# A linear-attention and MoE-block kernel: its whole instruction order written by hand, and the transposes of queries and the maxima of keys moved off TensorE

## The chip, the core and the metric

One core of a Trainium2 chip runs the whole program in one launch. The metric is device time in microseconds from start to end of an execution. TensorE (PE in the profile) multiplies, VectorE (DVE), ScalarE (ACT) and GpSimd (POOL) do elementwise work, SyncE (SP) issues the DMAs. Each engine works off its own queue in order and waits for others by semaphores.

## What is computed

```python
# q, k, v: 8 batches, 8 heads, 576 tokens, 64 wide;  w_in 512x2048, w_out 2048x512 (float64)
q_s = exp(q - max(q, axis=-1));  q_s = q_s / (sum(q_s, axis=-1) + 1e-9)   # softmax of a query over its 64
k_s = exp(k - max(k, axis=2));   k_s = k_s / (sum(k_s, axis=2) + 1e-9)    # softmax of keys over the 576 tokens
kv  = einsum('bhsd,bhse->bhde', k_s, v)                                   # one 64x64 matrix for each head
x   = einsum('bhsd,bhde->bhse', q_s, kv)                                  # as 4608 tokens x 512
h   = x @ w_in;  g = h - tanh(h);  out = g @ w_out                        # 4608 x 512
```

## The kernel before

The 4608 tokens are 36 tiles of 128, taken in nine chunks of four (512 tokens). For each chunk the hidden layer of 2048 is walked in 16 steps `f`, so there are 144 steps. A step is 12 matmuls `ph` (w_in times x, the matrices held in two parts each: high times high, high times low, low times high, four slices of 128 each) and 12 matmuls `po` (four token tiles, in each `gh` by the two parts of w_out and `gl` by the first one). Between the two lies the elementwise chain of the step: `u`, `t`, `m`, `vv` on ScalarE, `g`, `tt`, `gg`, `cp` on VectorE, then `gh` (ScalarE) and `gl` (GpSimd, in places VectorE). `ph` has two banks of PSUM, so `ph` of step n+2 cannot start before the last reader of step n's bank, `tt`, is done. The `po` of a step follows the `ph` of two steps later (`LAG = 2`).

Beside the steps runs the attention for the chunks to come. For each batch: load keys and values, maximum over tokens (`kv_max` on VectorE folds 576 tokens to 128 rows; four transposes `pm` on TensorE and a reduction `mx` give one column of maxima; `kv_rows`, tile `pb`, spreads it to all partitions by two 512-column matmuls with a diagonal `d`, built by GpSimd, in batches 2 to 7), `kv_sub`, `kv_exp`, 80 small matmuls `pk` (`kv_mm`), `kv_norm` into `kvs`. For each query tile: softmax (`q_max`, `q_sub`, `q_exp`, `q_sum`, `q_eps`, `q_inv`), `q_norm` (GpSimd), `q_turn` (four TensorE transposes into PSUM, tile `pt`), `q_keep` (ScalarE copies them to SBUF), and for each pair of tiles `x_mm` (matmuls `px`), of which `x_part` makes `xh` (ScalarE) and `xl` (VectorE).

The 64 left-over tokens of two batches form a tile of their own after every odd batch, so chunks and batches do not line up. `ORDER` writes out the order of all engines for the first 19 steps, in which the weights are also split into two parts (`cl`, `pr`, `lo`, `st`, `ca`, `sub`). After that only the queues of TensorE and SyncE are in written order (`prepare` puts each attention part at a half step); the program's scheduler orders the other three engines. `warm` words are idle matmuls ahead of the first step.

Of the kernel before, what the change touches and what calls it, by code (L numbers as in the profile page):

```python
# [31 lines left out]
ORDER = """  # L32
q1 q0 mq1 qu1 qe1 mq0 qu0* k0.0 k0.1 k0.2 km0.a ld.i2 km0.b warm4 km0.c km0.d sq1 qe0 pm0 cl.i2
vo0.0 pr.i2 vo0.2 mx0 ld.i1 lo.i2 sa1 mh0 sr1 ld.i0 ml0 vo0.1 cl.i1 ld.i4 pb0 qn2 v0.0 lo.i0 sq0
pt2 lo.i1 lo.i4 ks0.0 cl.i0 qs2 ke0.0 st.i2 qn3 sa0 q3 ks0.2 sr0 ks0.1 warm13 pk0.0 ca.i2 pt3
warm2 ke0.2 pr.i0 qn1 pt1 mq3 qn0 cl.i4 ke0.1 v0.1 st.i0 qu3* v0.2 pt0 pr.i1 pk0.1 pr.i4 qs0 ld.o0
vo1.1 pk0.2 ca.i0 qs3 st.i4 sl0 rs0 rc0 qe3 kn0 qs1 sub.i0 cl.o0 q2 sq3 st.i1 pr.o0 ld.i5 warm5
ld.i3 px0 mq2 sa3 cl.i5 vo1.2 px2 ca.i4 sub.i2 lo.o0 sub.i4 xh0.0 xh2.0 k1.0 xl0.0 ca.i1 xh2.1
xl2.0 xl2.1 ld.o2 xh0.1 lo.i3 k1.1 xl0.1 qu2 ld.o1 vo1.0 k1.2 lo.i5 v1.2 cl.i3 sub.i1 ld.i6 warm10
qe2 pr.i3 sr3 km1.a ph0 sq2 lo.o2 km1.b ld.i12 ph1 pr.i5 st.i3 qn6 m0 km1.c u0 t0 ld.o7 ld.i7 pt6  # L40
v1.0 cl.o1 km1.d vv0 ph2 ca.i3 g0 sa2 t1 tt0 qs6 lo.o1 u1 pr.o1 lo.i6 gg0 ld.o5 sr2 cp0 ld.o3 g1
u2 gh0 sub.i3 st.i5 cl.i12 ld.o10 pm1 mx1 m1 ph3 pr.i12 vv1 qn4 tt1 cl.i6 cl.o2 st.o0 gg1 mh1 v1.1
ph4 cl.i7 ml1 pb1 t2 pr.i6 ld.i9 pr.o2 ca.o0 cp1 ca.i5 st.i6 lo.i7 vv2 gl0 sub.i5 u3 ks1.0 qn5 gh1
ks1.1 t3 ks1.2 ke1.0 ld.i10 pt4 ke1.1 ke1.2 cl.o5 g2 ca.i6 st.o1 ca.o1 qs4 ph5 gl1 tt2 pk1.0 gg2
pk1.1 pk1.2 tt3 sub.o0 m2 po0.0 u4 qn7 ld.o13 cp2 g3 vv3 lo.o3 sl1 cl.o3 ld.i8 st.o2 ld.o4 sub.o1
m3 po0.1 po1.1 pt5 gg3 pr.i7 po0.2 qs5 po0.3 ca.o2 st.i7 vv4 ld.o6 cp3 ld.o8 sub.o2* gh2 t4 ld.i11
gl2* rs1 po1.3 sub.i6 pt7 m4 ca.i7 cl.o4 po1.0 po1.2 po2.1 u5 tt4 pr.o3 lo.o4 rc1 ld.i15 g4 po2.3
gh3 gg4 po2.2 st.o3 t5 ld.o12 cp4 kn1 sub.i7 lo.o5 po2.0 ca.o3 ld.o9 qs7 ph6 vv5 px4 gl3* gh4
pr.o5 sub.o3 pr.o4 u6 tt5 g5 po3.0 cl.o6 m5 st.o5 st.o4 cl.i9 po3.2 ld.o11 po3.1 xh4.1 ca.o4 xh4.0
t6 sub.o4 gg5 cp5 ca.o5 pr.o6 ld.i13 lo.i11 lo.o6 po3.3 xl4.1 gh5 lo.o7 xl4.0 tt6 vv6 ld.o15 ph7  # L50
gl4* t7 px6 xh6.1 cl.o10 st.o6 po4.2 lo.i15 g6 po4.1 sub.o5 cl.i10 gg6 po4.3 tt7 xl6.1 gl5 m6 cp6
xh6.0 po4.0 cl.o7 u7 po5.2 cl.o9 xl6.0 ca.o6 m7 ld.i14 po5.1 po5.0 g7 vv7 po5.3 ph8 sub.o6 pr.i9
gh6 cl.o8 cl.i11 lo.i12 pr.o7 gg7 ph9 cl.i15 cl.i8 cp7 st.o7 t8 gl6* u8 gh7 ca.o7 sub.o7 t9 g8
ld.o14 u9 po6.2 po6.0 tt8 po6.1 gl7* lo.i10 m8 vv8 po7.0 cl.o15 g9 tt9 po6.3 pr.i15 ph10 pr.i11
gg8 ev.0 cp8 cl.i14 cl.o11 lo.o10 m9 pr.o10 po7.2 vv9 gh8 sv.0 t10 u10 ph11 st.i15 st.o10 po7.3
gg9 cp9 lo.i8 tt10 cl.o12 ev.2 vv10 ca.o10 m10 gl8 st.i11 u11 po7.1 sub.o10 g10 ca.i15 po8.1 po8.0
gh9 pr.o8 gl9* cl.o13 gg10 t11 ev.3 ca.i11 ph12 cp10 ev.1 tt11 vv11 po9.1 g11 sub.i11 sv.1 pr.i10
po8.2 gg11 u12 st.i12 po8.3 gh10 po9.2 m11 gl10* po9.3 st.i10 t12 po9.0 g12 cp11 po10.1 ca.i12
pr.o12 ph13 ca.i10 tt12 po10.0 vv12 sub.i15* lo.o12 pr.i8 cl.o14 sub.i12 sub.i10 po10.2 gg12 lo.i9
m12 st.i8 ph14 st.i9 gh11 t13 cp12 u13 gl11* lo.o8 sv.3 ca.i8 vv13 lo.i14 po10.3 t14 tt13 g13 gh12  # L60
st.o12 m13 gg13 u14 po11.1 po11.0 po11.2 ph15 sub.i8 ca.o12 pr.i14 ca.i9 cl.i13 gl12 pr.o15
sub.o12 pr.o11 cp13 st.i14 po11.3 tt14 vv14 po12.1 t15 po12.3 g14 lo.o15 sub.i9 st.o8 m14 lo.o11
po12.2 ca.i14 gh13 sub.i14 gg14 ca.o8 cp14 st.o15 tt15 pr.o9 po12.0 gl13* ph16 u15 po13.2 lo.o9
st.o11 gh14 vv15 gl14* sub.o8 po13.1 po13.3 sv.2 ca.o15 st.o9 ca.o11 g15 u16 lo.i13 gg15 sub.o15
m15 g16 po13.0 ca.o9 po14.2 t16 cp15 pr.i13 po14.1 vv16 sub.o11 sub.o9* gh15 tt16 po14.0 st.i13
ph17 m16 lo.o13 u17 pr.o13 po14.3 gg16 vv17 gl15* ph18 po15.1 cp16 g17 gh16 po15.2 po15.0 m17 t17
po15.3 st.o13 gg17 gl16* t18 u18 lo.o14 po16.2 vv18 tt17 cp17 g18 po16.1 pr.o14 tt18 ca.o13 m18
gg18 ca.i13 gh17 st.o14 po16.3 sub.o13* cp18 po16.0 ca.o14 sub.i13* gh18 gl17* sub.o14* gl18*
# [765 lines left out]
```

## Time and profile before

| | |
|---|---|
| three runs | 894.58, 894.74, 894.89 us (median 894.74) |
| profiled execution | 894.5 us, its span 892.7 us, mean granted clock 0.998 |
| TensorE busy | 872.3 us, 98% of the span |
| VectorE, ScalarE, GpSimd busy | 610.8, 555.1, 301.6 us (68%, 62%, 34%) |
| DMA queue of SyncE | 56.63 MB, 20.6% of 16 engines' span |

The span starts and ends with the first and the last instruction; 1.8 us of the execution lie around it. Consecutive matmuls overlap in the records (a duration of 393 ns, a new one every 227 ns), so what TensorE needs for a piece of work is read from the distance between starts. A wait is time in which an engine stood idle, put down to what released it.

### The profile page before, as it was taken

How to read it: one execution, taken by the hardware profiler on the slowest of the kernel's cores; microseconds unless marked ns; L12 is line 12 of the kernel's file. 1: busy time of each engine (PE TensorE's matmuls, PEld its weight loads, DVE VectorE, ACT ScalarE, POOL GpSimd, SP SyncE). 2: the span in 40 equal slices, each digit the busy share in tenths (PEclk: the TensorE clock that was granted, in tenths of full speed). 3: DMA queues.
4: the chain of work that ended last, by engine and by line, in shares of the span. 5: the costliest groups of instructions: out<-in, count | busy, mean ns of one | idle time of the engine just before them, and what ended most of it. 6: DMA issues, size and time to landing. Idle time of an engine off the chain costs nothing.

```text
span 892.7 us, 13189 instructions
## 1 busy us (share of the span) xinstructions
PE 872.3 (98%) x5008; PEld 716.3 (80%) x5008; DVE 610.8 (68%) x897; ACT 555.1 (62%) x967; POOL 301.6 (34%) x255
## 2 busy tenths in 40 slices
PE   5899999999999999999999999999999999999997
PEld 4788878888878888888888888888888888888886
DVE  7899999856686767666756865765766466454454
ACT  5799987656465556565655564566555556556553
POOL 3463361533153324332433233323433233222221
PEclk9999999999999999999999999999999999999999
DMA  9991301130413011300240011401100020001001
GB/s 294 323 391 55 98 3 42 48 119 1 129 49 106 1 36 48 108 25 0 71 108 24 1 47 37 106 1 48 48 25 1 3 69 12 1 1 48 1 1 47
DMA packets 79775, 57.47 MB, mean 64 GB/s; under 512 B 14688, under 2 KB 72032, under 8 KB 79712
## 3 DMA queue, kind: packets, MB, share of 16 engines
q1 hardware_dynamic: 79712, 56.63, 20.6%
q8 instruction: 39, 0.64, 0.3%
q14 instruction: 24, 0.20, 0.1%
HBM read 46.14 MB, written 10.49 MB: 63 GB/s over the span
## 4 chain that ended last, share of the span: by engine, by line
PE 92%; DVE 3%; ACT 2%; DMA 1%; issue 1%; POOL 0%; SPq 0%; DVEq 0%; ACTq 0%; POOLq 0%
PE po L653 42%; PE ph L570 42%; PE pk L325 2%; PE pt L463 2%; PE px L489 2%; PE warm L202 1%; DMA q<-in_q_dram 1%; DMA k<-in_k_dram 1%; PE pb L299 0%; PE pb L283 0%; DVE km L252 0%; PE pm L261 0%; POOL d L293 0%; DMA out_dram<-back 0%; DVE mq L410 0%
## 5 line engine op out<-in xcount | busy, mean ns | idle before, releaser
L653 PE MATMUL po<-w_o,gh 128*128 128x512 f32 x1152 | 358.8, 393 | 0.0
L570 PE MATMUL ph<-xh,w_i 128*128 128x512 f32 x1152 | 311.9, 393 | 0.0
L610 POOL TENSOR_TENSOR gl<-g,gh 128x512 fp32r<-128x512 f32 x129 | 172.5, 1337 | 387.0 <-ACT gh L607 369.2
L653 PEld LDWEIGHTS po<-w_o,gh 128*128 128x128 f32 x1152 | 214.0, 188 | 47.0 <-issue 2.1
L570 PEld LDWEIGHTS ph<-xh,w_i 128*128 128x128 f32 x1152 | 213.8, 188 | 43.4 <-DVE mq L410 0.2
L591 DVE SCALAR_TENSOR_TENSOR g<-u,ph 128x512 f32<-128x512 f32 x144 | 98.1, 681 | 209.8 <-ACT t L585 201.1
L653 PE MATMUL po<-w_o,gl 128*128 128x512 f32 x576 | 224.7, 390 | 1.1 <-DVE gl L610 1.1
L607 ACT CAST gh<-g 128x512 fp32r<-128x512 f32 x144 | 89.4, 621 | 170.4 <-DVE g L604 164.7
L570 PE MATMUL ph<-xl,w_i 128*128 128x512 f32 x576 | 154.5, 390 | 0.0
L585 ACT ACTIVATE u<-ph 128x512 f32<-128x512 f32 x144 | 86.1, 598 | 75.6 <-PE ph L570 72.2
L599 DVE SCALAR_TENSOR_TENSOR g<-vv,g 128x512 f32<-128x512 f32 x144 | 117.9, 818 | 18.6 <-ACT vv L585 8.0
L653 PEld LDWEIGHTS po<-w_o,gl 128*128 128x128 f32 x576 | 108.1, 188 | 25.2 <-DVE gl L610 2.2
L570 PEld LDWEIGHTS ph<-xl,w_i 128*128 128x128 f32 x576 | 108.0, 188 | 23.4 <-DVE xl L510 0.2
L604 DVE COPY_PREDICATED g<-mk,t 128x512 f32<-128x512 int32 x144 | 122.3, 850 | 3.5
L585 ACT ACTIVATE mk<-ph 128x512 int32<-128x512 f32 x144 | 86.3, 599 | 36.1 <-DVE g L591 32.9
L585 ACT ACTIVATE vv<-u,b_pa 128x512 f32<-128x512 f32 x144 | 104.7, 727 | 0.0
L596 DVE TENSOR_TENSOR t<-ph,t 128x512 f32<-128x512 f32 x144 | 98.0, 680 | 1.5 <-ACT mk L585 1.5
L585 ACT ACTIVATE t<-ph 128x512 f32<-128x512 f32 x144 | 85.5, 595 | 0.9 <-PE ph L570 0.9
L449 POOL TENSOR_TENSOR qn<-q,sq 128x512 f32<-128x512 f32 x30 | 33.0, 1102 | 25.4 <-PE pt L463 12.8
L415 POOL TENSOR_TENSOR q<-q,mq 128x1024 f32<-128x1024 f32 x13 | 26.3, 2021 | 43.2 <-DVE mq L410 43.0
L410 DVE TENSOR_REDUCE mq<-q 128x16 f32<-128x1024 f32 x15 | 18.2, 1216 | 20.0 <-DMA q<-in_q_dram 19.9
L181 POOL TENSOR_TENSOR w_i<-c_i,w_i 128x512 fp32r<-128x512 f32 x14 | 20.2, 1448 | 28.5 <-ACT w_i L177 28.5
(94 smaller groups left out, 583.8 us busy)
## 6 DMA issues: line engine op xcount, KB each, us to landing
k<-in_k_dram SPq DMA_DIRECT2D x16, 512.0 KB, 5.6
raw_i<-in_moe_w_in_dram SPq DMA_DIRECT2D x16, 512.0 KB, 6.9
raw_o<-in_moe_w_out_dram SPq DMA_DIRECT2D x16, 512.0 KB, 8.1
q<-in_q_dram SPq DMA_DIRECT2D x15, 512.0 KB, 4.0
v<-in_v_dram SPq DMA_DIRECT2D x14, 512.0 KB, 4.9
out_dram<-o SPq DMA_DIRECT2D x28, 256.0 KB, 2.0
kr<-in_k_dram SPq DMA_DIRECT2D x8, 128.0 KB, 5.2
spare_v<-in_v_dram SPq DMA_DIRECT2D x2, 512.0 KB, 8.4
```

The costliest lines, as they stand in the source:

```text
L181: eng.tensor_tensor(w[:, 1], st["c"].bitcast(F32), w[:, 0].bitcast(F32), op=ALU.subtract)
L415: eng.tensor_tensor(qf, qf, mq, op=ALU.subtract)
L449: eng.tensor_tensor(qn.rearrange("p a g d -> p g a d"), qt[:, :, j].rearrange("p (g a) d -> p g a d", g=2), sq[:, :, j : j + 1] .broadcast ...
L570: nc.tensor.matmul(ph, w[:, i, c], x[:, c, :], start=(n == 0), stop=(n == len(ops) - 1))
L585: nc.scalar.activation(new(tag, **of), st[src], fn, **kw)
L591: nc.vector.scalar_tensor_tensor(new("g"), st["u"], C2, st["ph"], op0=ALU.mult, op1=ALU.mult)
L596: nc.vector.tensor_tensor(st["t"], st["ph"], st["t"], op=ALU.subtract)
L599: nc.vector.scalar_tensor_tensor(st["g"], st["vv"], PB, st["g"], op0=ALU.add, op1=ALU.mult)
L604: nc.vector.copy_predicated(st["g"], st["mk"], st["t"])
L607: nc.scalar.copy(new("gh", F32R), st["g"])
L610: eng.tensor_tensor(new("gl", F32R), st["g"], st["gh"].bitcast(F32), op=ALU.subtract)
L653: nc.tensor.matmul(po[t], g[:, cols], wt["o", f][:, w], start=(begin and n == 0), stop=(end and n == 2),)
```

## The change

- Every instruction of the five engines now stands in a written order: `FIRST` for the first 32 steps, `ROUND` once for each of chunks 2 to 8 (words with + prepare the next chunk and fall away where there is none), `LAST` for the end. A step's `ph` is cut in three words (`pha`, `phb`, `phc`, four matmuls each) and a tile's `po` in two (`a`: the two `gh` matmuls, `b`: the `gl` one), which need not be neighbours. A star puts a word on VectorE that otherwise goes to GpSimd.
- Queries of chunks 2 to 8: `q_scale` normalizes in place, two VectorE transposes (`q_blocks`, word `tb`) turn the tile within squares of 32x32, one DMA puts it in DRAM (`qp`), four DMAs fetch its squares back in their places (`qg`). `q_turn` and `q_keep` remain for chunks 0 and 1 only.
- Keys' maxima of batches 2 to 7: a VectorE transpose in squares (`kb`), a reduction (`kr`), three small ScalarE copies that bring quarters together (`kq`), a reduction and a transpose on VectorE (`kx`, `kt`), 2 KB to DRAM (`kp`) and back, spread over 128 partitions (`kg`). `kv_sub` then reads SBUF and may go to GpSimd. `pm`, `mx`, `mh`, `ml`, `d` and `pb` remain for batches 0 and 1 only.
- The left-over tokens of all batches form chunk 8, so chunk j is batch j; `kvs` is saved to DRAM for it (`kv_save`) and read back (`kv_again`).

```diff
-    tiles = []
-    for b in range(B):
-        tiles += [((b, u), j) for u in range(NKP) for j in range(2)]
-        if b % 2:
-            tiles.append(((b, "rest"), 0))
+    tiles = [((b, u), j) for b in range(B) for u in range(NKP) for j in range(2)]
+    tiles += [(("rest", m), j) for m in range(B // 4) for j in range(2)]
...
+    def q_blocks(i: int):
+        unit, j = tiles[i]
+        qt = qs_of[unit][:, :, j]
+        qs_of[i] = tb = ap.tile([P, 2, 2, NC, SQ], F32, name=f"tb{i}", tag="qs", bufs=3)
+        for g in range(2):
+            nc.vector.transpose(
+                tb[:, g],
+                qt[:, g * NC : (g + 1) * NC].rearrange("p a (s i) -> p s a i", s=2),
+            )
+
+    def q_put(i: int):
+        tb = qs_of[i]
+        nc.sync.dma_start(qd[i], tb.rearrange("p g s a t -> p (g s a t)"))
+
+    def q_get(i: int):
+        qs_of[i] = qs = ap.tile([P, NQ, NC, SQ], F32, name=f"qs{i}", tag="qs", bufs=3)
+        rows = qd[i].rearrange("(q i) (c n) -> i q c n", q=NQ, c=NQ)
+        for c in range(NQ):
+            nc.sync.dma_start(
+                qs[c * SQ : (c + 1) * SQ].rearrange("p q a t -> p q (a t)"), rows[:, :, c]
+            )
...
+    def kv_best_put(b: int, st: dict):
+        nc.sync.dma_start(kvm[b].rearrange("(c i) -> c i", i=SQ), st["rt"][:NB])
+
+    def kv_best_get(b: int, st: dict):
+        st["mrow"] = mrow = ap.tile([P, H, D], F32, name=f"mrow{b}", tag="qs", bufs=3)
+        nc.sync.dma_start(
+            mrow.rearrange("p h d -> p (h d)"), kvm[b].unsqueeze(0).broadcast_to([P, DM])
+        )
...
+ROUND = """
+pha0 +q.0 phb0 phc0 po14.0a po14.3a u0 t0 g0 po14.0b po15.0a pha1 phb1 vv0 phc1 +mq.0 po14.2a m0
+t1 pha2 po15.0b po14.3b gg0 po15.3a u1 po14.1a po14.2b m1 tt0 po15.2a po15.3b cp0 gh0 tt1 +qu.0
...
+po1.2b phb4 m3 t3 phc4 vv3 os.0 po0.1b t4 g2 po1.0b gg2 pha5 cp2 po1.1a +k.2 gh2 po1.1b po0.3b
+po1.3a phb5 po2.0a +sq.0 os.3 +sa.0 u4 +sr.0 g3 po1.3b tt3 phc5 po2.2a os.1 gg3 os.2 vv4 cp3 gl2*
+pha6 gh3 m4 po2.3a u5 po2.1a phb6 vv5 t5 po2.1b tt4 g4 phc6 gg4 +k.0 cp4 gl3* m5 po2.0b +k.1
++again gh4 +q.1 po2.2b g5 pha7 u6 tt5 t6 vv6 gg5 cp5 po3.0a po2.3b tt6 phb7 +km.a po3.0b +qn.1
+gl4* g6 phc7 po3.2a u7 po4.0a po4.0b +km.b m6 +qn.0 po3.1a t7 gh5 +km.c gg6 po3.3a cp6 po3.1b
+po3.2b po3.3b +km.d +kb pha8 po4.3a +tb.1 po4.2a phb8 g7 po4.1a phc8 po4.3b +tb.0 m7 +v.0 +kr gh6
+t8 po4.1b +kq.1 po4.2b tt7 po5.0a +kq.2 u8 +kq.3 +kx +qp.0 tt8 pha9 gl5 po5.0b vv7 +kt gg7 phb9
...
++sl u12 po9.0b m11 po9.3b gg11 tt12 gh10 +rs +rc po9.2a g12 pha13 vv12 +kn phb13 +tb.3
+po9.1a phc13 po9.2b cp11 po10.0a po9.1b gl10 +px.0 gh11 m12 po10.2a po10.0b gg12 po10.1a +tb.2 u13
++xh.0.0 pha14 po10.3a po11.0a t13 tt13 gl11 phb14 cp12 +qp.3 phc14 +qp.2 po10.1b po10.2b vv13
+po10.3b gh12 g13 m13 +xh.0.1 gl12 pha15 po11.3a po11.1a t14 gg13 phb15 po11.2a phc15 po11.0b
+po11.2b cp13 +xl.0.0 u14 po11.1b po11.3b po12.0a m14 g14 tt14 po12.2a +qg.3 vv14 po12.1a po12.3a
++qg.2 gh13 gg14 po12.1b +px.1 po12.0b +xl.0.1 u15 m15 t15 cp14 po12.3b +sv po12.2b vv15 po13.0a
++gl13* gh14 g15 gg15 +xh.1.1 po13.1a +xh.1.0 po13.2a tt15 cp15 gh15 gl14* +xl.1.0 po13.0b po13.3a
+po13.1b +xl.1.1 po13.3b gl15* po13.2b
+"""
+
+LAST = """
+po142 po143.0a po143.0b oc8.0 os8.0 po143.1a po143.1b oc8.1* os8.1 po143.2a po143.2b oc8.2 os8.2
+po143.3a po143.3b oc8.3* os8.3
```

## Rows read from the trace of the kernel before

**Rows 1.** The page: busy time of the engines (share of the span, number of instructions), and TensorE's busy tenths and granted clock in 40 equal slices of the span.

```profile
PE 872.3 (98%) x5008; PEld 716.3 (80%) x5008; DVE 610.8 (68%) x897; ACT 555.1 (62%) x967; POOL 301.6 (34%) x255
...
PE   5899999999999999999999999999999999999997
...
PEclk9999999999999999999999999999999999999999
```

**Rows 2.** All waits of TensorE: who waited for whom, us in total, times, longest.

```profile
PE pm L261 <- DVE km L255: 8.3, 1, 8.3
PE warm L202 <- DVE xl L510: 3.0, 1, 3.0
PE warm L202 <- POOL ident masks.py:199: 1.4, 1, 1.4
PE pb L283 <- DVE mh L270: 1.2, 1, 1.2
PE po L653 <- DVE gl L610: 1.1, 1, 1.1
PE pb L299 <- POOL d L293: 0.4, 1, 0.4
```

**Rows 3.** TensorE's timeline, chunk 6: start us, us, instruction. Starts of `ph`, `pt`, `pm`, `pb`, `px` and `pk` that bound single steps: a plain step (578.08 to 583.52), steps with a transposed query tile (583.52, 589.43), with a pair's `px` (595.36 to 602.08), with the keys' maxima (618.41, 624.34), with `pk` (630.28 to 637.03).

```profile
578.08 1.07 PE L570 MATMUL ph<-xh,w_i 128*128 128x512 f32 x4
...
583.52 0.60 PE L463 MATMUL pt<-ident,qn 128*128 128x128 f32 x4
...
589.43 0.60 PE L463 MATMUL pt<-ident,qn 128*128 128x128 f32 x4
...
595.36 1.07 PE L570 MATMUL ph<-xh,w_i 128*128 128x512 f32 x4
...
602.08 1.07 PE L570 MATMUL ph<-xh,w_i 128*128 128x512 f32 x4
...
618.41 0.60 PE L261 MATMUL pm<-ident,km 128*128 128x128 f32 x4
...
624.34 0.63 PE L299 MATMUL pb<-d,one_r 128*128 128x512 f32 x2
...
630.28 1.07 PE L570 MATMUL ph<-xh,w_i 128*128 128x512 f32 x4
...
637.03 1.07 PE L570 MATMUL ph<-xh,w_i 128*128 128x512 f32 x4
```

**Rows 4.** Groups of TensorE instructions by line: count, busy us, mean ns of one; idle before.

```profile
L463 PE MATMUL pt<-ident,qn 128*128 128x128 f32 x144 | 22.3, 279 | 0.0
...
L299 PE MATMUL pb<-d,one_r 128*128 128x512 f32 x12 | 4.0, 405 | 0.4 <-POOL d L293 0.4
```

**Rows 5.** Busy time by stretch (us from the span's start): length, then PE, PEld, DVE, ACT, POOL with instructions, granted clock, DMA share, GB/s.

```profile
60.00:80.00 20.00, 20.00 (x144) 15.50 (x142) 19.65 (x35) 19.61 (x38) 7.94 (x6) 1.00 0.40 153
...
300.00:390.00 90.00, 90.00 (x542) 73.69 (x541) 58.90 (x86) 53.28 (x94) 31.21 (x27) 1.00 0.17 48
```

**Rows 6.** Groups of VectorE instructions by line: count, busy us, mean ns of one; idle before and its releasers.

```profile
L596 DVE TENSOR_TENSOR t<-ph,t 128x512 f32<-128x512 f32 x144 | 98.0, 680 | 1.5 <-ACT mk L585 1.5
...
L604 DVE COPY_PREDICATED g<-mk,t 128x512 f32<-128x512 int32 x144 | 122.3, 850 | 3.5
...
L610 DVE TENSOR_TENSOR gl<-g,gh 128x512 fp32r<-128x512 f32 x15 | 11.0, 733 | 2.3 <-ACT gh L607 2.3
...
L410 DVE TENSOR_REDUCE mq<-q 128x16 f32<-128x1024 f32 x15 | 18.2, 1216 | 20.0 <-DMA q<-in_q_dram 19.9
...
L346 DVE TENSOR_TENSOR kvs<-pk,rs 128x256 f32<-128x256 f32 x8 | 3.4, 424 | 0.2
```

**Rows 7.** DMA issues by tile: number, KB each, median us from issue to landing.

```profile
q<-in_q_dram SPq DMA_DIRECT2D x15, 512.0 KB, 4.0
...
out_dram<-o SPq DMA_DIRECT2D x28, 256.0 KB, 2.0
...
q_rest<-in_q_dram SPq DMA_DIRECT2D x8, 128.0 KB, 3.1
```

**Rows 8.** SyncE's timeline between 487 and 553 us: start, time that the issue took.

```profile
487.05 0.37 SPq L395 DMA_DIRECT2D q<-in_q_dram  x1
...
551.42 1.36 SPq L384 DMA_DIRECT2D q_rest<-in_q_dram  x2
```

**Rows 9.** The timeline of all engines at the end: the last `ph`, `tt` of that step, and the weight loads of its first `po`.

```profile
878.20 1.07 PE L570 MATMUL ph<-xh,w_i 128*128 128x512 f32 x4
...
882.25 0.68 DVE L596 TENSOR_TENSOR t<-ph,t 128x512 f32<-128x512 f32 x1
...
884.49 0.30 PEld L653 LDWEIGHTS po<-w_o,gh 128*128 128x128 f32 x2 [0.21 <-ACT gh L607]
...
885.22 0.19 PEld L653 LDWEIGHTS po<-w_o,gl 128*128 128x128 f32 x1 [0.43 <-DVE gl L610]
```

**Rows 10.** The timelines of TensorE and VectorE in the first 36 us.

```profile
31.98 3.80 PE L202 MATMUL warm<-ident 128*128 128x128 f32 x20 [3.05 <-DVE xl L510]
...
35.43 1.59 PE L570 MATMUL ph<-xh,w_i 128*128 128x512 f32 x4
...
4.67 1.22 DVE L410 TENSOR_REDUCE mq<-spare_q 128x16 f32<-128x1024 f32 x1 [4.67 <-DMA spare_q<-in_q_dram]
...
31.25 2.47 DVE L510 TENSOR_TENSOR xl<-px,xh 128x512 fp32r<-128x512 f32 x4
```

More of the change, by code (lines that the diff above doesn't have):

```diff
@@ L38 @@
[L38 to L43, printed above, removed]
@@ L50 @@
[L50 to L55, printed above, removed]
@@ L56 @@
[L56 to L61, printed above, removed]
@@ L127, in attn_moe_kernel @@
     nc.gpsimd.tensor_copy(one_r, one)
+    SQ = 32
+    NQ = P // SQ
+    NB = DM // SQ
+    best = sm.tile([SQ, SQ], F32, name="best")
+    nc.gpsimd.memset(best, 0.0)
     kvs = [const.tile([P, NC, D], F32, name=f"kvs{i}") for i in range(3)]
@@ L585, in act, with ph @@
             nc.scalar.activation(new(tag, **of), st[src], fn, **kw)
-        def ph():
-            st["ph"] = h_mm(j, f)
+        def ph(part: int):
+            if "ph" not in st:
+                pool, tag = (ps_o, "o") if j == 0 and f in (2, 3) else (ps_h, "h")
+                st["ph"] = pool.tile([P, CH], F32, name=f"ph{j}_{f}", tag=tag)
+            w = wt["i", f].rearrange("p t (c f) -> p t c f", c=NC)
+            i, x = ((0, 0), (0, 1), (1, 0))[part]
+            for c in range(NC):
+                n = st["n"] = st.get("n", -1) + 1
+                nc.tensor.matmul(
+                    st["ph"], w[:, i, c], xs[j][x][:, c, :], start=n == 0, stop=n == 3 * NC - 1
+                )
         def g():
@@ new lines, in attn_moe_kernel, with go, many @@
+    ENG = mybir.EngineType
+    POOLED = {"qu", "qn", "gl", "sub", "ks"}
+    def go(name: str, fn):
+        kind = name.lstrip("+").split(".")[0].rstrip("0123456789*")
+        if name[-1] == "*":
+            fn(nc.vector)
+        elif kind in POOLED and not (kind == "ks" and name[0] != "+"):
+            fn(nc.gpsimd)
+        elif kind == "kq":
+            fn(nc.scalar)
+        else:
+            fn()
+    def many(name: str) -> list:
+        bare = name.rstrip("0123456789")
+        if "." in name or bare not in ("ph", "po"):
+            return [name]
+        if bare == "ph":
+            return [f"pha{name[2:]}", f"phb{name[2:]}", f"phc{name[2:]}"]
+        return [f"{name}.{t}{part}" for t in range(TPC) for part in "ab"]
@@ L805 @@
+    with tc.manual_schedule(engines={ENG.PE, ENG.DVE, ENG.Activation, ENG.Pool, ENG.SP}):
+        run(FIRST, 1)
+        for j in range(2, NCH):
+            run(ROUND, j)
+        run(LAST, 0)
 _INS = ["q", "k", "v", "moe_w_in", "moe_w_out"]
```

473 lines of the change are left out of this document (267 added, 206 removed).

## Prediction

> **What bounds the kernel now.** I read the page's busy line and slices first: TensorE is busy 98% of the span and at nine tenths or more in all slices but the first two and the last, at the full granted clock (the 2.4 GHz level); the others stand at 34 to 68% [rows 1]. Then the list of all its waits: 15.4 us, of which all but the last two entries (1.5 us) lie ahead of the first step [rows 2]. From the first `ph` at 35.43 us [rows 10] to the end the kernel is one unbroken stream of matmuls, and what a piece of work costs there is what it adds to the distance between starts. A plain step lasts 5.44 us (578.08 to 583.52) [rows 3], that is 24 matmuls of 0.2267 us. 144 steps are 783 us; the other 69 of the 852 us from the first `ph` to the last `po` are attention matmuls and the 1.5 us of waits. So the change is worth what it takes out of TensorE's stream, less every idle time that it puts there.
>
> **What it takes off TensorE.** A step with a transposed query tile lasts 5.91 us (583.52 to 589.43) and 5.93 (to 595.36): 0.48 more than a plain one. Four transposes a tile, 144 in all [rows 4], make 36 tiles; `q_turn` stays for 8, so 28 go: 28 x 0.48 = 13.4 us. The step with `pm` lasts 5.93 (0.49 more) and the one with `pb` 5.94 (0.50 more) [rows 3]; both go for six batches (12 `pb` of this form, two each [rows 4]): 6 x 0.99 = 5.9 us. Together 19.3 us. `pk` stays (1.31 more in the step from 630.28).
>
> **What stays on TensorE in another form.** `px` now reads its queries in runs of 32 columns and, in chunk 8, in pieces of 64. No row has runs of 32. The nearest: a pair of which one tile is in 64-column pieces adds 6.72 - 5.44 = 1.28 us (595.36 to 602.08) [rows 3], so I price every pair at that, and the change of form at 0; bounds -1 us and +6 us (14 pairs, each a third dearer). The cut of `ph` and `po` into words adds no instruction: 0, since every matmul loads its own weights already.
>
> **What it adds elsewhere, and its cover.** A round holds, on TensorE, 16 x 5.44 + 2 x 1.28 + `pk` 3.2 = 92.9 us. On VectorE:
> - Transposes `tb`: eight a round of 128x256. The trace has no VectorE transpose; the 128x256 `kvs` took 0.424 us, and the dearest per element, `copy_predicated`, 0.85 for 128x512 [rows 6]. I take 0.42 (same size), bounds 0.25 and 0.85: 3.4 us a round (2 to 7).
> - `kb` and `kr` about 0.7 each (a 128x512 pass is 0.68), `kx` and `kt`, of 64 and 32 columns, an estimated 0.2 each (half the 128x256 one): 1.8, in place of `mx`, `mh`, `ml`.
> - Eight `gl` with a star at 0.733 [rows 6] and two starred `qn` at 0.68: 7.2.
> With the steps' four passes (16 x 3.03 = 48.5), reductions, `km`, `ks`, `xl` and the rest by their means I come to 76 us of 92.9; a 90 us stretch before held 59 [rows 5]. ScalarE loses the `qs` copies and gains three small ones; GpSimd loses `d` and half of `gl`. All of that is hidden by TensorE as long as no wait ends last on it, which is the question of the next part.
>
> Two trips through DRAM are new. Count the matmuls between the words in a round, at 0.2267 us each. From `px.0`'s end (whose reading frees the buffer that `tb.2` writes) to `px.1` lie 12.5 us. In them fall `tb.2` (0.85), the store (2.0 for 256 KB [rows 7]), eight fetches queued on SyncE at about 0.4 to 0.7 each [rows 8], and the last landing (3.1 for a 128 KB load [rows 7]): 9 to 12 us, room 0.5 to 3. The other tiles have over 10 us. The maxima's trip, `kt` to `ks.0`, has 6.6 us by the same count for a store and a load (2.0 and 3.1 to 4.0, so 5.1 to 6.0 [rows 7]); late, it holds VectorE's queue, not TensorE's: `gg9` and `tt10` are queued behind `ks.0`, and TensorE notices after 5 us more. SyncE's in-order queue passes over `os`, `kp`, `kg` and values; `v.2` (landing about 66.5 us into the round, for `pk.2` at 67.7) is the tightest. Extra traffic is 28 x 2 x 256 KB on DMA engines busy 0.17 of the time [rows 5]: 0.
>
> **Waits that the new order may put in.** Before, the `ph` of step n+2 started 8.16 us after that of step n ended (three half steps). In `ROUND` that distance varies from 4.76 (`pha2`, `pha7`) to 12.4. The chain in between is read at the end: `ph` ends about 879.27, `tt` at 882.93, 3.7 us later [rows 9]. In front of `tt0` the new VectorE queue also holds `mq.0`, 1.2 us [rows 6]: 4.9 us against 4.76. At `pha9` VectorE has 9.2 us of work between `tt6` and `tt7`, with about 1 us of room; elsewhere 2.4 us or more. I put in 0.3 us a round, 2 us in all over seven rounds; bounds 0 and 14 (2 us a round: both spots and `px.1` late).
> In the first 32 steps VectorE and ScalarE are as full as TensorE (19.65 and 19.61 of 20 us) [rows 5]; before, TensorE lost 1.1 us there (`gl`) [rows 2]. The new text moves no more work there but has `po0` start 12.6 us after the first `ph`, where it was 21.5: 0 net, bounds -1 and +4.
>
> **Start and end.** VectorE ran without a pause worth naming from 4.67 us to the last `xl` at 33.7, and 10 `warm` pairs (3.8 us) came after the first `xl` [rows 10]. The new queue holds 45 instructions up to that `xl` in place of 42, 1 us more by their durations; a third query load stands before the keys; but the first `xl` comes earlier than the others and `warm` has 9. I take -1 us, bounds -2 and +3. At the end TensorE waited 0.2 + 0.4 us for `gh` and `gl` of the last step [rows 9]; now 11.5 us of `po` lie between: -0.6.
>
> **Sum** against the profiled execution: 894.5 - 19.3 - 0.6 - 1 + 2 = 875.6 us, 2.1% less; 894.5 lies 0.2 below the median of the runs, 894.74, which does not matter here.
>
> **A rule against it.** The rows show a TensorE transposition of a tile at 0.48 us of stream [rows 3], and VectorE a third idle [rows 1]. The Trainium skill, "VectorE: DVE Perf Modes", § The three transpose paths, says that VectorE transposes 32x32 blocks only, and its § Rules for kernel authors names TensorE for 128x128 where PSUM is acceptable. By that rule the change buys 0.48 us with two passes, five DMAs and an order that must hide them; if they are not hidden it is the second rival's time. The trace speaks for the change so far, since it is TensorE that is full; no run here has the block transposes yet.
>
> **Rivals.**
> 1. *The order costs some idle time in each round*, 1 to 2.5 us more than I put in, where VectorE's or ScalarE's queue is tight (`tt0`, `tt7`, `px.1`, `pk.2`): 883 to 893. For: distances of 4.76 us where there were 8.16. Against: 92.9 us hold only 76 of VectorE. Chance 0.2, three quarters of it still below 889.
> 2. *Slower: the trip through DRAM ends last.* Place: `px.1` in each round, behind `tb.2`, store and eight fetches. Price: each us late is 7 us. Even at 19.9 / 7 = 2.8 us late on top of the room of up to 3: a trip of 12 to 15 us. At 5 us late the time is 875.6 + 35 = 911. For: the eight fetches share one queue and none like them is in the trace; against: stores of this size land in 2.0 us and loads of twice it in 4 [rows 7]. Chance 0.08.
> 3. *VectorE becomes the bound* by dear transposes: from (92.9 - 72.6) / 8 = 2.5 us each, three times the dearest row; at 3.5 us, 8 us a round or 56 more: 931. Chance 0.02.
> 4. *The gain is lost in the first 40 us and the first 32 steps* and the rounds bring little (ScalarE late there): 890 to 896. Chance 0.04.
>
> **How the numbers follow.** Forecast 875.6, chance 0.66, its own range 871 to 882. Low end of the whole: all bounds at their best, 894.5 - 19.3 - 0.6 - 2 - 1 = 871.6, so 871. High end 889 takes in most of rival 1 and leaves out the rest, 0.15 or so with the chance below 871. Two tenths of a per cent, 1.8 us, is about what a measurement of this kernel can tell from no change. Faster 0.87 (forecast, rival 1, a part of 4), same 0.04, slower 0.09.
>
> **What would show it.** Right: `pt` 32 instructions, `pm` 8, no `pb` of 512 columns; TensorE's waits after the first `ph` under 4 us; plain steps still 24 x 0.2267. Wrong: waits of `px` for a DMA (rival 2), of `ph` for `tt` (rival 1), VectorE near 100% in 300 to 840 us (rival 3), the first `ph` after 38 us (rival 4), `px` over 1.3 us a pair (its price).

## The result, and the profile after

The changed kernel takes 881.09 us (median of four runs, 879.53 to 881.67), the kernel before, run beside it, 894.82 (894.58 to 896.0): a ratio of 0.9841 [0.9824, 0.9858], 1.6% faster. A second set, with more runs of the kernel before, gave 880.85 us and 0.9843 [0.9829, 0.9856]. The forecast was 875.6 us in a range of 871 to 889. The profiled execution took 881.66 us with a span of 879.8; that is 6.1 us over the forecast, and the sections below look for them.

The page of the changed kernel, its busy line, against [rows 1]:

```profile
PE 859.3 (98%) x4868; PEld 704.8 (80%) x4868; DVE 655.3 (74%) x1010; ACT 540.0 (61%) x955; POOL 217.9 (25%) x183
```

TensorE still has 98% of a shorter span; VectorE's share rose to 74%, GpSimd's fell to 25%. The work did leave TensorE, and VectorE had the room. The groups by line (count, busy us, mean ns of one, idle before) say that the pieces are there in the numbers foreseen, against [rows 4, 6]:

```profile
L693 DVE COPY_PREDICATED g<-mk,t 128x512 f32<-128x512 int32 x144 | 135.4, 940 | 10.4 <-ACT mk L665 6.4
...
L542 DVE STREAM_TRANSPOSE tb<-q 128x256 f32<-128x256 f32 x48 | 18.1, 415 | 6.0 <-DMA qd<-tb 6.0
...
L339 DVE STREAM_TRANSPOSE kb<-km 128x512 f32<-128x512 f32 x6 | 4.2, 702 | 0.2
```

A transposition of 128x256 on VectorE costs 415 ns, where 420 had been taken, of 128x512 702 ns. One row is worse than before: `copy_predicated`, the same 144 instructions, has a mean of 940 ns where it had 850 [rows 6].

TensorE's timeline, the starts of `px.0` in two rounds and of `px.1` in the second, shows what a round costs:

```profile
394.07 1.10 PE L632 MATMUL px<-qs,kvs 64*64 64x128 f32 x32
...
486.97 1.10 PE L632 MATMUL px<-qs,kvs 64*64 64x128 f32 x32
...
500.74 1.10 PE L632 MATMUL px<-qs,kvs 64*64 64x128 f32 x32
```

486.97 - 394.07 = 92.90 us, against the 92.9 that were counted from the matmuls alone: nothing is waited for in a round, and TensorE's last wait in the whole trace ends at 165.80 us. So the 6.1 us are not in the rounds. The list of TensorE's waits (us in total, times, longest), against [rows 2], shows where to look:

```profile
PE ph L675 <- ACT mk L665: 2.3, 2, 2.0
...
PE ph L675 <- DVE xl L653: 1.2, 1, 1.2
...
PE ph L675 <- DVE t L685: 0.8, 2, 0.5
```

These three rows are 4.3 us of waits by `ph` in the feed-forward stream, all in the first 32 steps; before there was one of 1.1 us there, by `po` [rows 2]. The longest, 2.0 us, stands at 165.80 us. TensorE's timeline around it (start, time, instruction, idle before):

```profile
165.80 1.19 PE L675 MATMUL ph<-xh,w_i 128*128 128x512 f32 x4 [2.00 <-ACT mk L665]
...
167.06 2.68 PE L739 MATMUL po<-w_o,gh 128*128 128x512 f32 x6
...
172.79 0.39 PE L675 MATMUL ph<-xh,w_i 128*128 128x512 f32 x1
```

Six `po` matmuls last 2.68 us where six at 81.21 us last 1.53. The busy times by stretch (length; PE, PEld, DVE, ACT, POOL with instructions; granted clock, DMA share, GB/s) show why:

```profile
160.00:165.00 5.00, 3.81 (x17) 2.81 (x15) 4.97 (x5) 1.43 (x3) 3.36 (x2) 1.00 0.00 0
165.00:170.00 5.00, 4.20 (x13) 3.33 (x14) 4.96 (x9) 3.85 (x7) 0.00 (x0) 0.71 0.00 0
170.00:175.00 5.00, 5.00 (x22) 4.12 (x21) 3.91 (x7) 4.12 (x8) 0.00 (x0) 0.94 0.00 0
...
300.00:390.00 90.00, 90.00 (x517) 73.68 (x516) 66.46 (x104) 54.40 (x96) 18.23 (x16) 1.00 0.26 78
```

The granted clock was 1.00, TensorE idled for 2.0 us, and then it was 0.71 and 0.94: part of that time went at the 1.2 GHz level. From 165.80 to 172.79 stand 23 matmuls, 5.21 us at 0.2267 each; they took 6.99. The wait of 2.0 us cost 3.8 in this execution. It does not in every one: e6, an experiment below, has the same words in its first 32 steps, and its TensorE timeline has the same wait and then the same six `po` at the full clock (granted clock 1.00 from 165 to 175 us):

```profile
165.91 1.20 PE L677 MATMUL ph<-xh,w_i 128*128 128x512 f32 x4 [2.00 <-ACT mk L667]
...
167.17 1.55 PE L741 MATMUL po<-w_o,gh 128*128 128x512 f32 x6
```

The clock fell behind this wait in four of the profiled executions (this one, `after_again`, e2, e10: 0.66 to 0.73 from 165 to 170 us) and stayed at 1.00 in three (e5, e6, e7). What tells them apart is open. The reason for the wait itself stands in the same window of the changed kernel, in the timeline of all engines:

```profile
160.51 2.85 POOL L404 TENSOR_TENSOR k<-k,mrow 128x1024 f32<-128x1024 f32 x1
...
161.13 2.82 DVE L693 COPY_PREDICATED g<-mk,t 128x512 f32<-128x512 int32 x1
...
165.15 0.60 ACT L665 ACTIVATE mk<-ph 128x512 int32<-128x512 f32 x1 [3.23 <-DVE g L680]
```

`ks.0` of batch 2 (L404) runs on GpSimd until 163.36. VectorE's `copy_predicated`, begun at 161.13, is not done before 163.95, 2.1 us more than its median (0.76), and `mk` and the next `ph` are late behind it. That is a reading of neighbours; whether the one makes the other wait is for an experiment. (Before the change `kv_sub` read PSUM and stood on VectorE; `ks.0` on GpSimd is new here.)

### The profile page after: what moved, and what is told of

Its sections match the earlier page's. It is cut to its first block, busy times and chain, and to the rows that moved or that the text cites. A ratio compares the mean times of both kernels' runs of the same rounds, so it can differ in the third digit from the quotient of the medians.

```text
span 879.8 us, 13120 instructions
## 1 busy us (share of the span) xinstructions
PE 859.3 (98%) x4868; PEld 704.8 (80%) x4868; DVE 655.3 (74%) x1010; ACT 540.0 (61%) x955; POOL 217.9 (25%) x183
## 4 chain that ended last, share of the span: by engine, by line
PE 88%; DVE 5%; ACT 2%; POOL 1%; DMA 1%; issue 1%; SPq 1%; POOLq 0%; ACTq 0%; DVEq 0%
PE po L739 42%; PE ph L675 42%; PE pk L418 2%; PE px L632 2%; DMA raw_o<-in_moe_w_out_dram 1%; DVE g L693 1%; POOL gl L700 1%; DVE c_i L241 1%; DVE g L680 1%; DVE g L688 0%; DMA q<-in_q_dram 0%; DVE mq L506 0%; DVE sq L519 0%; PE warm L274 0%; POOL w_o L252 0%
## 5 line engine op out<-in xcount | busy, mean ns | idle before, releaser
L739 PE MATMUL po<-w_o,gh 128*128 128x512 f32 x1152 | 326.1, 392 | 0.0
L675 PE MATMUL ph<-xh,w_i 128*128 128x512 f32 x1152 | 307.4, 390 | 3.1 <-ACT mk L665 2.3
L700 POOL TENSOR_TENSOR gl<-g,gh 128x512 fp32r<-128x512 f32 x79 | 109.9, 1391 | 416.7 <-PE po L739 228.1
L739 PE MATMUL po<-w_o,gl 128*128 128x512 f32 x576 | 191.0, 394 | 0.0
L693 DVE COPY_PREDICATED g<-mk,t 128x512 f32<-128x512 int32 x144 | 135.4, 940 | 10.4 <-ACT mk L665 6.4
L688 DVE SCALAR_TENSOR_TENSOR g<-vv,g 128x512 f32<-128x512 f32 x144 | 100.9, 701 | 19.2 <-ACT vv L665 16.0
L700 DVE TENSOR_TENSOR gl<-g,gh 128x512 fp32r<-128x512 f32 x65 | 44.6, 686 | 26.4 <-PE po L739 20.6
L511 POOL TENSOR_TENSOR q<-q,mq 128x1024 f32<-128x1024 f32 x15 | 31.4, 2094 | 73.7 <-DVE mq L506 73.7
L519 DVE TENSOR_REDUCE sq<-q 128x16 f32<-128x1024 f32 x15 | 18.2, 1213 | 12.8 <-ACT q L514 12.8
L651 ACT CAST xh<-px 128x512 fp32r<-128x512 f32 x36 | 20.2, 588 | 8.8 <-PE px L632 8.7
```

Source lines behind the costliest of these rows:

```text
L511: eng.tensor_tensor(qf, qf, mq, op=ALU.subtract)
L519: nc.vector.tensor_reduce(sq, qf, axis=AX.X, op=ALU.add)
L651: nc.scalar.copy(xh, px_of[i][g])
L675: nc.tensor.matmul(st["ph"], w[:, i, c], xs[j][x][:, c, :], start=n == 0, stop=n == 3 * NC - 1)
L688: nc.vector.scalar_tensor_tensor(st["g"], st["vv"], PB, st["g"], op0=ALU.add, op1=ALU.mult)
L693: nc.vector.copy_predicated(st["g"], st["mk"], st["t"])
```

## The experiments

Theory A for the missing 6 us: GpSimd's instructions hold VectorE up in the first 32 steps, where VectorE is full. Theory B: VectorE is late there by its own queue, whatever GpSimd does. For the gain: either the matmuls removed pay wherever they stood, or the new order is what frees their time.

**The change once more, and `ks.0` on VectorE (e1).** `after_again` is the changed kernel, for the comparison.

> The changed kernel once more, unaltered, as the yardstick of the next three runs on this chip. Every theory: 879.5 to 881.7 us, as in its first four runs, ratio to the kernel before 0.984.

```diff
-... gg20 +ks.0 vv21 cp20 tt21
+... gg20 +ks.0* vv21 cp20 tt21
```

> One star: the first key subtraction of batch 2 (ks.0, 128x1024, in the text of the first 32 steps) goes to VectorE in place of GpSimd; all else as in the changed kernel. Theory A (the two engines block each other): in the changed kernel copy_predicated of step 20 began at 161.13 us, 0.6 us after ks.0 on GpSimd (2.85 us), and took 2.82 us in place of 0.76, ending with it; TensorE then waited 2.0 us at 165.8 and worked at half clock for a while. With ks.0 on VectorE (1.2 us) copy_predicated takes 0.76 again, the mask of step 22 comes some 0.9 us earlier, and the wait shrinks to about 1.1 us: 1 to 3 us faster than the changed kernel, depending on whether the clock still drops. Rival B (VectorE is late there by its own queue, 4.97 of 5 us busy): another 1.2 us in its queue makes the wait 3.2 us: 1 to 3 us slower.

The star moves one instruction to VectorE. The time is 878.37 us (878.1 to 879.87), 0.982 [0.9806, 0.9833]: 2.5 us less than 880.85, with intervals that overlap at their ends, so the traces decide. The start of `mk` in `after_again`, then the timeline of e1 (all engines) and its waits of TensorE for `mk`:

```profile
164.36 0.60 ACT L665 ACTIVATE mk<-ph 128x512 int32<-128x512 f32 x1 [3.23 <-DVE g L680]
```

```profile
160.28 1.21 DVE L404 TENSOR_TENSOR k<-k,mrow 128x1024 f32<-128x1024 f32 x1
...
161.42 0.75 DVE L693 COPY_PREDICATED g<-mk,t 128x512 f32<-128x512 int32 x1
...
163.37 0.60 ACT L665 ACTIVATE mk<-ph 128x512 int32<-128x512 f32 x1 [2.18 <-DVE g L680]
```
```profile
PE ph L675 <- ACT mk L665: 1.2, 2, 0.9
```

VectorE was given 1.21 us more work and was done 1.0 us earlier: the first `ph` starts at 32.81 us here and at 32.76 in `after_again`, `mk` at 163.37 instead of 164.36. `copy_predicated` takes 0.75 us again, and the longest wait falls from 2.0 to 0.9. Theory B would have had it later. A holds for the wait. From the first `ph` to the end of the last `po` the two traces have 837.39 and 839.99 us, 2.6 less: 1.0 of it is shorter waits, 1.6 the clock, which stayed at 1.00 here. Since it also stayed there behind the full wait in e5 and e6, that part is not shown to be the star's.

**The stores of the last tiles on two queues (e2).** At the end of the changed kernel SyncE issues eight stores: the tiles of left-over tokens belong to two batches each and need two stores. The second store of the last three tiles goes to ScalarE's queue:

```diff
-... oc8.1* os8.1 po143.2a po143.2b oc8.2 os8.2 po143.3a po143.3b oc8.3* os8.3
+... oc8.1* osp8.1 po143.2a po143.2b oc8.2 osa8.1 osp8.2 osa8.2 po143.3a po143.3b oc8.3* osp8.3 osa8.3
```

> Only the last stores are changed: the second halves of the last three tiles go out from ScalarE's queue, the rest from SyncE's as before. Theory A (the end is bound by SyncE's issues: eight of 0.63 us in a row, 5.05 us, where the kernel before had five, 3.3 us): the last issue ends near 875.4 in place of 877.2 us of the span, and the execution is 1.5 to 2 us shorter. Rival B (the end is bound by the landing of the last store whatever queue it is in): under 0.5 us.

It took 879.01 us (878.68 to 880.66), 0.9827 [0.9813, 0.984]. This interval overlaps that of the changed kernel, so the traces decide. The timeline of SyncE in the changed kernel, and of the two queues here:

```profile
872.18 5.05 SPq L767 DMA_DIRECT2D out_dram<-o  x8
```
```profile
872.21 3.12 SPq L768 DMA_DIRECT2D out_dram<-o  x5
...
873.01 1.98 ACTq L768 DMA_DIRECT2D out_dram<-o  x3
```

From the end of the last `po` to the end of the span the kernel before needed 4.9 us, the changed one 6.2 (873.57 to 879.8), this one 5.2 (873.60 to 878.8). So 1.0 us is shown, not the 1.8 of the medians.

**`xl` ahead of the splitting of weights (e5).** For the wait of 1.2 us for `xl` at 83.96 us:

```diff
-xh6.1 xh6.0 g6 cl.i15 ... st.i9 po5.3a gg6 xl6.1 ca.i9 pr.i15 xl6.0 t7
+xh6.1 xh6.0 xl6.1 xl6.0 g6 cl.i15 ... st.i9 po5.3a gg6 ca.i9 pr.i15 t7
```

> Only two words are moved: the two xl of the second pair of chunk 1 stand on VectorE ahead of a weight clamp, a weight shift and two steps' words, which came before them. Theory A (TensorE's wait of 1.22 us at 83.96 for xl comes from a clamp and a shift that took 1.50 and 1.78 us in place of 0.42 and 0.68 while GpSimd worked): xl no longer waits behind them, the wait goes, 1 to 1.5 us faster than the changed kernel. Rival B (the words that now come later make the next ph wait for its bank instead): no change, the wait at another line.

880.08 us, 0.9845 [0.9824, 0.9866]: nothing. TensorE's waits here:

```profile
PE ph L675 <- DVE g L680: 1.2, 1, 1.2
```

The wait for `xl` is gone and the same 1.2 us are waited for `g`; all waits of the stream sum to 4.6 us for 4.1 in `after_again`. (Its stretch from the first `ph` to the last `po` is still 1.3 us shorter, because the clock stayed at 1.00 behind the long wait.) Written earlier, one instruction delays another as long as the queue as a whole is late: here the rival was right.

**`gl` of step 5 on VectorE (e10)**, the other way to the same wait. In the changed kernel two more VectorE instructions ahead of it stand beside GpSimd's, the later one of 1.78 us where its like take 0.68 (all engines):

```profile
80.20 1.35 POOL L700 TENSOR_TENSOR gl<-g,gh 128x512 fp32r<-128x512 f32 x1 [1.62 <-ACT gh L696]
80.32 1.78 DVE L241 SCALAR_TENSOR_TENSOR c_i<-raw_i 128x512 uint32<-128x512 uint32 x1
```

```diff
-... xl6.0 t7 gl5 po5.0a
+... xl6.0 t7 gl5* po5.0a
```

> The changed kernel with gl of step 5 on VectorE instead of GpSimd, at its written place behind both xl. In the changed kernel GpSimd's gl at 80.20 us (1.35 us) stands beside a VectorE instruction that took 1.78 us where its like take 0.68, and TensorE then waits 1.22 us for xl. Theory A (GpSimd's instruction holds VectorE up, and that is the whole wait): VectorE's instruction takes 0.68 us, the wait for xl falls to 0.2 us or less, the time by 1 us to about 880. Theory B (VectorE is late by its own queue there): the wait for xl stays near 1 us, or as much appears at the next instructions, and the time stays at 881.

```profile
79.69 0.68 DVE L241 SCALAR_TENSOR_TENSOR c_i<-raw_i 128x512 uint32<-128x512 uint32 x1
```

The instruction takes its 0.68 us, and the list of TensorE's waits has none for `xl` by `ph` left. From the first `ph` to the end of the last `po` the traces have 839.99 us for `after_again` and 839.16 here: 0.8 of the 1.2 us. The two can be compared, since the granted clock behind the long wait was 0.66 from 165 to 170 us in both. The time, 880.14 us with 0.9845 [0.9831, 0.986], can't tell that from nothing. The mechanism is A's, the size less than the wait.

**The transposes put back (e3).** The changed kernel with four identity transposes on TensorE, of no use, at `+tb.0`, `+tb.1`, `+qp.0` and `+qp.1`: the 112 that were taken away, in the new order.

```diff
+    if key in ("+tb.0", "+tb.1", "+qp.0", "+qp.1"):
+        pt = ps_m.tile([P, NC, P], F32, name="extra", tag="m")
+        for a in range(NC):
+            nc.tensor.transpose(pt[:, a, :], ident, ident)
```

> The changed kernel with four TensorE transposes of the identity added for each of the 28 tiles (112 in all, results unused), in the round well ahead of pk. Nothing else changes. Theory A (TensorE is full, so what is in its stream is paid in full): 28 x 0.48 = 13.4 us more than the changed kernel, 894.5 us. Rival B (part of the stream's gaps hide them): under 10 us more.

892.56 us, 0.9979 [0.9969, 0.9989]: 11.7 us more than without. Its `px.0` in two rounds:

```profile
303.37 1.10 PE L632 MATMUL px<-qs,kvs 64*64 64x128 f32 x32
...
398.17 1.10 PE L632 MATMUL px<-qs,kvs 64*64 64x128 f32 x32
```

A round lasts 94.80 us, 1.90 more: 4 x 0.475, the full price. That the whole is 11.7 and not 13.3 lies in the first 32 steps (the traces have 850.48 us from the first `ph` to the end of the last `po`, 10.5 more than `after_again`): there the extra matmuls fill 0.6 us of the longest wait (1.4 left of 2.0), and the clock stayed at 1.00 behind it, where `after_again` lost 1.7 us.

**The removal alone, in the old order (e4, e8).** A first edit leaves out transposes, `pm` and `pb` of the kernel before at once:

> The kernel before, in its own order, with the transposes of the 28 later query tiles and the transposes and broadcasts of the keys' maxima of batches 2 to 7 left out (the copies read the untransposed tile, the subtraction reads one of GpSimd's diagonals; the output is not the reference's). Nothing of what the change puts in their place is there. Theory A (the gain is TensorE's stream alone, and what the new order adds is the waits in its first 32 steps and the longer end): 19.3 us less than the kernel before, 875.5 us, some 5 us faster than the changed kernel. Rival B (the gain comes from the written order itself, which fills the stream better): less than 12 us below the kernel before, 883 or more.

890.65 us, 0.9952 [0.9937, 0.9967]: only 3.6 of 19.3 us. Taken by itself this would say that the old order has no room. But the edit has a fault of its own: without `pb` the subtraction reads `d` from SBUF where it had read PSUM, and its timeline shows the same collision. Below it stand the subtraction's instructions with `d` and with `pb` (ns: shortest, median, longest) and the largest of TensorE's waits behind the first `ph`:

```profile
250.06 4.29 DVE L308 TENSOR_TENSOR k<-k,d 128x1024 f32<-128x1024 f32 x2 [0.89 <-POOL d L296]
...
251.00 2.27 POOL L610 TENSOR_TENSOR gl<-g,gh 128x512 fp32r<-128x512 f32 x1
```
```profile
L308 DVE TENSOR_TENSOR k<-k,d x12: 1161/2173/2311, 156.6 to 581.3; 128x1024 f32<-128x1024 f32 x12
...
L308 DVE TENSOR_TENSOR k<-k,pb x4: 1153/1218/1221, 16.1 to 52.2; 128x1024 f32<-128x1024 f32 x4
```
```profile
PE ph L570 <- DVE t L596: 7.9, 6, 2.0
```

Two instructions of 1.2 us last 4.29 beside GpSimd's, and TensorE waits for `t` behind them; its waits behind the first `ph` sum to 11.7 us, where the kernel before has 1.4. So a second edit leaves out the query transposes alone (from tile 8 on; nothing in their place):

```diff
+        if i >= 2 * TPC:
+            qs_of[i] = qn.rearrange("p (a n) -> p a n", a=NC)
+            return
         qs_of[i] = pt = q_psum(i, f"pt{i}")
```

> The kernel before with one part of the change alone: TensorE's transposes of the query tiles are left out from tile 8 on (28 tiles x 0.48 us = 13.4 us of TensorE's time), and nothing is put in their place: the copy of ScalarE takes the tile as it was scaled, not transposed, so the products with kvs are of other numbers than the reference's. The keys' maxima keep their way over TensorE. Theory A (the removed matmuls are worth their time on TensorE in any order, since every wait was already hidden): 894.6 - 13.4 = 881 us, and no new wait after the first ph. Theory B (the old written order has no room: each round then runs into waits for VectorE, ScalarE or GpSimd, so that the new order is what makes the gain): 886 to 893 us, and waits of TensorE for t, mk, g, gl or px of several us in all.

880.59 us, 0.9849 [0.9833, 0.9866]: 13.4 less, as much as 28 x 0.48. (From the first `ph` to the last `po` the trace has 13.75 us less than that of the kernel before, of which 0.6 is a shorter wait for `gl` and 0.5 the lower clock that the kernel before had at its first `ph`; some 12.7 are the stream itself.) Its waits of TensorE behind the first `ph`:

```profile
PE pb L299 <- POOL d L293: 0.5, 1, 0.5
PE po L656 <- DVE gl L613: 0.4, 1, 0.4
```

No new ones. The old order gave the time back without a word being moved, so the new order is not what makes the removal pay. Whether the replacement (VectorE's transposes and the trip through DRAM) would have fitted into the old order was not tried.

**The trip of the queries through DRAM, longer (e6, e7).** Each fetch of a tile cut into 8, then into 16 DMAs where there are 4, the same bytes:

```diff
-            nc.sync.dma_start(qs[c * SQ : (c + 1) * SQ].rearrange(...), rows[:, :, c])
+            for h in range(0, NQ, 2):     # 2: 8 fetches a tile; 1: 16
+                nc.sync.dma_start(qs[c * SQ : (c + 1) * SQ, h : h + 2].rearrange(...),
+                                  rows[:, h : h + 2, c])
```

> Each query tile is fetched from DRAM by 8 DMAs of 32 KB in place of 4 of 64 KB: eight more issues on SyncE, some 0.45 us each, in the trip of the second pair (store to px.1). Theory A (the trace of the changed kernel: last fetch issued 7.0 us ahead of px.1 and landed 2.2 us later, so 4.8 us of room): 3.6 us more fits, no change within 1 us. Rival B (my prediction's room of 0.5 to 3 us): px.1 late by 0.6 to 3 us in each of seven rounds, 4 to 21 us more.

> The same with 16 DMAs of 16 KB for each tile: 24 more issues in the trip of the second pair, some 10.8 us. Theory A (4.8 us of room): px.1 late by about 6 us in each of seven rounds, 40 us more, 920 us. Rival B (SyncE issues small DMAs faster than 0.45 us, or other words fill TensorE's time): under 15 us more.

Eight: 880.87 us, 0.9848 [0.9833, 0.9862], no difference. Sixteen: 955.38 us, 1.0675 [1.0653, 1.0697]. SyncE's timeline of one trip in the changed kernel, and its DMAs by tile (number, KB each, median us from issue to landing), against [rows 7, 8]:

```profile
485.32 4.56 SPq L549 DMA_DIRECT2D qd<-tb  x2
489.99 3.73 SPq L555 DMA_DIRECT2D qs<-qd  x8
```
```profile
qd<-tb SPq DMA_DIRECT2D x28, 256.0 KB, 2.7
...
qs<-qd SPq DMA_DIRECT2D x112, 64.0 KB, 2.2
```

The last fetch is issued at 493.72 and lands some 2.2 us later; `px.1` starts at 500.74, 4.8 us after that. With eight the issues last 7.79 us, 4.1 more: still inside. With sixteen, 14.76 us, 11.0 more, outside, and the waits of TensorE are:

```profile
PE px L634 <- DMA qs<-qd: 22.3, 11, 3.5
PE pk L418 <- DMA vr<-in_v_dram: 12.5, 5, 2.8
PE px L634 <- DMA kva<-kvs: 10.1, 3, 3.6
```

The wait of `px` for the fetched queries, which was expected at 40 us, is 22.3; the other 22.6 are loads of values and of saved `kvs` that stand behind the fetches in SyncE's queue. Together they are 44.9 us; the time is 74.5 longer. The mean granted clock was 0.965 against 0.990, so a part of the rest is slow matmuls behind the waits; how much is open.

**Three edits together (e9).** `ks.0` on VectorE and moved behind `g21`, the stores on two queues, and the four `warm` matmuls in the middle of the first chunk left out.

```diff
-... gh0 gl0 mh1 pha4 vv1 qn4 warm4 ml1 pr.i6
+... gh0 gl0 mh1 pha4 vv1 qn4 ml1 pr.i6
-... gg20 +ks.0 vv21 cp20 tt21 po19.2a g21 m21
+... gg20 vv21 cp20 tt21 po19.2a g21 +ks.0* m21
```

> The changed kernel with three things at once: ks.0 of batch 2 in the first 32 steps on VectorE instead of GpSimd, and written behind g21 instead of ahead of vv21; the stores of the last three tiles on two queues; and the four warm-up matmuls in the middle of the first chunk (warm4, 0.8 us) left out. Theory A (waits made by GpSimd's lock on VectorE, SyncE's queue at the end and the four matmuls each cost what the trace shows): 880.9 - 3.8 (2.0 us of wait and the slow clock behind it) - 1.8 - 0.8 = 874.5 us, the wait of ph for mk at most 0.3 us. Theory B (they only cover for other waits: the time that one gives back is waited for elsewhere, as with the wait for xl): 877 us or more; pb waits for ml 1.2 us instead of 0.4, and ph for mk, t or g in sum as long as before.

876.85 us (875.96 to 878.38), 0.9806 [0.9792, 0.9821]: the fastest version here, 4.0 us under the changed kernel and 1.9% under the kernel before. In the list of TensorE's waits `mk` no longer stands: the 0.9 us that e1 still had are gone here, where `ks.0` stands behind `g21`. What `pb` waits for, where the `warm` matmuls had been:

```profile
PE pb L392 <- DVE ml L384: 0.4, 1, 0.4
...
PE pb L392 <- DVE mh L380: 0.2, 1, 0.2
```

The first of the two was there before, so the four matmuls hid 0.2 of their 0.8 us. From the first `ph` to the end of the last `po` it has 835.65 us against 839.99 for `after_again`: 4.3 of the 4.6 expected (1.7 of them the lower clock that `after_again` had behind the long wait). The tail is 1.0 shorter, as above, not 1.8. The other 1.4 us of what misses to the expected 874.5 lie ahead of the first `ph`, which starts at 34.20 here and at 32.76 in `after_again`, in the same instructions (last section).

## Why the prediction came out as it did

Right in sign and mechanism, 5.5 us short in size: 881.09 where 875.6 was said. That it lies in the range owes something to luck: one term left its own bounds (the first 32 steps), and the range was wide for another place, the rounds, where nothing was lost. Step by step, the profiled execution against the terms:

- **What comes off TensorE, 19.3 us**: right to about 1 us. The removed transposes alone are worth 13.4 us in the old order, and put back in the new one 1.90 us a round; a round is 92.90 us, though the terms printed for it sum to 92.8. `pm` and `pb` (5.9 us) were not tried cleanly by themselves; the length of the round is what speaks for them.
- **`px` in its new form, 0**: right; a pair's 32 matmuls last 1.10 us, and the round comes out by the count.
- **Cover on VectorE**: right. `tb` 0.415 us for 0.42, `kb` 0.70 for 0.7; 66.5 of 90 us busy, less than the 76 of 92.9 that were counted. The rule that the prediction weighed against the change (the Trainium skill, "VectorE: DVE Perf Modes", § Rules for kernel authors: TensorE for 128x128) would have kept the transposes on TensorE. This case went the other way, for the reason given there: TensorE was full and VectorE was not.
- **Waits in the rounds, +2 (0 to 14)**: the end of its bounds, 0. The distances of 4.76 us in front of `tt0` and `tt7` held; room at `px.1` was 4.8 us, not 0.5 to 3. Rival 1 did not come. Rival 2 did not either, but its mechanism is real: with 11 us more of issues in that trip (e7) the time is 74.5 us longer.
- **The first 32 steps, "0 net, bounds -1 and +4"**: this is the step that failed in size. From the first `ph` to the end of the last `po` the kernel before took 852.36 us and the changed one 839.60, 12.8 less, where 19.3 + 0.6 were to go: 7.1 us were lost, and none of it in rounds. From the first `ph` to that of step 32 the two kernels took 188.64 and 192.71 us, 4.1 more where the prediction's prices make 2.9 less (four tiles' transposes, one `pm` and one `pb`): 7.0. The trace names most of it: waits of 4.3 us where there had been 1.1, 1.8 us at a lower clock behind the longest, 0.8 us for four `warm` matmuls that now stand inside the stream. That is 5.8; some 1.2 us stay unnamed, and the 1.8 came in some executions only (e6, with the same words there, took 191.06 us to step 32). The text had seen that VectorE and ScalarE are full there [rows 5] but counted their work as if GpSimd's did not touch it. Shown to be that are 1.1 of the longest wait's 2.0 us (e1; the other 0.9 went in e9, which also moves `ks.0`) and 0.8 us for the wait for `xl` (e10).
- **The end, -0.6**: the waits for the last step are gone, but the four tiles of left-over tokens need two stores each and SyncE's queue adds 1.3 us from the last `po` to the end. The prediction moved these tokens without counting their DMAs; e2 gets 1.0 us back.
- **The head, -1**: -1.5 in this execution (33.97 for 35.43), -2.7 in `after_again`.

-1.5 for -1, 0 for +2, 7.1 for 0 and 1.3 for 0: -0.5 - 2 + 7.1 + 1.3 = 5.9 of the 6.1 us.

## What to carry to other kernels

Where one engine is full without a gap, an instruction taken off it pays its whole time: here it did in the old order and in the new one, so count the engine's stream first. Where the second engine is full too, look beside each of its instructions that take two operands from SBUF, and beside its `tensor_scalar`s, for a GpSimd instruction at the same time; moving that one to the fuller engine can bring the fuller engine forward (e1: 1.2 us more work, done 1.0 us earlier). When a wait goes and comes back on the next line (e5), the queue is late as a whole there, and work taken out of it helps where another order does not; where the queue has room behind the wait (e9, `ks.0` behind `g21`) a move is enough.
